# A new order of the same steps on five engines, in a kernel that joins a recurrence to a two-layer network

## Chip, core and metric

One core of a Trainium2 chip runs the kernel. The metric is the device time of one execution in microseconds (us). Engines are named as in the profile: PE is TensorE (matmul) and PEld its weight loads, DVE is VectorE, ACT is ScalarE, POOL is GpSimd, SP issues the transfers.

## What is computed

The recurrence runs over 768 time steps for 4 x 8 heads of width 48, and its output, 3072 tokens of 384 numbers, goes through a two-layer network:

```python
state = np.zeros((B, H, D, D), dtype=np.float32)
for t in range(S):
    kt, vt, rt = (k[:, :, t], v[:, :, t], r[:, :, t])
    cur = np.einsum('bhd,bhe->bhde', u[None] * kt, vt)
    y[:, :, t] = np.einsum('bhd,bhde->bhe', rt, state + cur)
    state = w[None, :, :, None] * state + np.einsum('bhd,bhe->bhde', kt, vt)
...
h = x @ w_in                                         # 3072 x 384 by 384 x 2048
sp = np.maximum(h, 0.0) + np.log1p(np.exp(-np.abs(h)))
return ((h * erf(sp)) @ w_out).astype(np.float32)    # by 2048 x 384
```

## The kernel before

**Tiling.** The recurrence is cut into chunks of 128 time steps: 24 chunks, number g = 4 x (place in the sequence) + batch. Four chunks fill a block of 512 tokens, x. The network takes a block in 16 hidden tiles of 128, so 96 pairs of a first product (f0 to f95) and a second one (p0 to p95). The first two blocks go through hidden tiles 0 to 7 first, then both through 8 to 15. Products are made of three float32r passes (high and low parts), so f and p are 9 matmuls each.

**Order.** Nothing is scheduled by the framework: a string of some 1700 words, ORDER, is read from left to right, and each word issues one step. Each engine runs its own instructions in the order in which they were issued, and waits at an instruction until its inputs are there; buffers are handed out in that order too. A word is a letter, a number and, for some, a part; + at its end puts the step on GpSimd, * on ScalarE, nothing on VectorE.

- For chunk g: L (a, b) issue its two loads on SP (L66, L69). K and R multiply k and r in place by powers of the decay (L187, L191), V turns k on TensorE, N brings it back or multiplies k in its other layout (L195, L208). Q a and b multiply by u and by k (L212, L215), Q c sums to q (L219); M puts q on the diagonal of am for one half (L230 on ScalarE, L232 elsewhere). A is the k-r product (L249), P the masked copies of A into am (L255), Y the chunk's y (L272), D its contribution to the state (L291), S the state's update (a, b add: L303, L305; c, d scale: L309), X the high and low part of y written to the block's x (L312, L315).
- For weights: F fetches a group of 768 columns (two hidden tiles) of the first (0) or second (1) matrix, as 64-bit numbers, into one of two buffers (L102); C a to f make float32 of it and split it into a high and a low part: a, e on ScalarE (L118, L128), b, c, d on VectorE (L120, L122, L125), f the low part (L130). Group 13 is group 3 of the second matrix.
- For pair n: f (L338), a and b two tanh (L345, L349), z (L354), c, d, e (L358, L362, L366), g (L370), h the high part gh (L376), l the low part gl (L381), p (L397). h tiles have three buffers, s1, s2, gh and gl two each.
- W issues dummy matmuls that keep TensorE busy (L87), O moves a finished or interrupted accumulation out (L414 to L425), Z tests whether w lies in the expected range (L435 to L438), for a branch at the end.

The words are read by one loop:

```python
for i, x in enumerate(words):
    eng = {"+": nc.gpsimd, "*": nc.scalar}.get(x[-1], nc.vector)
    what, x = x[0], x.rstrip("+*")
    ...
    if what == "l":
        act_l(num, eng)
```

Of the kernel before, what the change touches and what calls it, by code (L numbers as in the profile page):

```python
# [619 lines left out]
Q6c N6+ z0 M61* M60+ P51 a1 C01f W4 Y5 c0 b1 S3a R6 C02a f2 z1 X5a C02b c1 X5b d0 C02c d1 A6 e0 C02d a2 P61 e1 F03  # L620
C02e g0 W4 D6 b2 P60 C02f+ f3 h0 g1 h1 l0 C11a Y6 z2 a3 C11b c2 C11c b3 f4 X6a S6b d2 l1 e2 C11d p0 a4 S6a S6d+ F12 g2
C11e S6c+ z3 b4 C11f c3 p1 h2 X6b C03a l2 d3 C03b f5 z4 e3 C03c c4 d4 C03d D5 e4 p2 S5a a5 F13 g4 S5c+ C03e S5b g3
S5d+ b5 C03f h3 D4 h4 l3 f6 L7a C12a S4a l4+ S4b z5 L7b c5 C12b f7 a6 S4c C12c d5 L8a b6 R7 e5 K7 L9a p3 a7 C12d b7
Q7a C12e F05 Q7b A7 C12f+ Q7c g5 M71* L9b z6 p4 M70* K9+ P71 L8b c6 K8+ P70 h5 Y7 d6 R9 C13a l5 e6 p5 z7 X7a Q8a+ g6
c7 X7b h6 Q8b d7 f8 l6 e7 C13b g7 N8+ Q8c h7 C13c A9 a8 M80* l7 f9 R8 b8 C13d z8 M81+ C13e F14 f10 c8 C13f a9 d8 Q9a
p6 b9 N7 S4d e8 z9 Q9b+ C05a g8 c9 p7 C05b h8 Q9c d9 N9 C05c O70a e9 f11 O70b M91+ O72a g9 a10 O72b M90+ P91 h9 b10
f12 l8+ P90 a11 O71a b11 l9+ O71b z10 A8 c10 C05d a12 d10 p8 z11 F04 C05e P80 c11 C05f+ P81 e10 Y9 d11 g10 b12 e11 h10
D8 g11 f13 C14a l10+ C14b z12 f14 a13 C14c c12 b13 C14d d12 p9 a14 F15 C14e e12 C14f b14 p10 g12 h11 C04a l11 z13 p11
h12 C04b c13 l12 d13 z14 e13 f15 C04c c14 C04d d14 e14 g13 F06 p12 C04e g14 a15 C04f h13 b15 f16 l13 h14 z15 C15a l14
c15 C15b f17 a16 C15c d15 b16 C15d e15 p13 a17 g15 F07 C15e z16 b17 C15f c16 f18 h15 C06a l15+ d16 p14 a18 z17 e16  # L630
C06b b18 C06c c17 p15 d17 C06d O150a g16 C06e O150b f19 h16 F16 C06f e17 O151a l16+ g17 C07a O151b f20 h17 C07b a19
l17 O152a z18 b19 O152b p16 C07c c18 a20 z19 d18 C07d c19 p17 e18 F17 d19 g18 b20 h18 f21 e19 l18+ C07e g19 h19 C07f+
z20 p18 a21 c20 b21 l19 C16a p19 z21 d20 C16b c21 C16c e20 d21 f22 g20 e21 C16d h20 g21 C16e f23 l20 h21 C16f a22 b22
l21 C17a p20 z22 a23 C17b c22 C17c b23 p21 d22 C17d e22 z23 C17e g22 f24 c23 C17f+ h22 d23 e23 l22 O232a f25 a24 g23
O230a b24 h23 z24 X9a l23 p22 c24 X9b a25 d24 b25 p23 e24 z25 O230b c25 g24 O230c d25 h24 Y8 O232b e25 l24+ O232c g25
f26 X8a S8b S8a h25 S8d+ X8b S8c+ l25+ O231a f27 a26 b26 z26 c26 D7 O231b a27 f28 L10a S7b d26 S7d S7a b27 L11a S7c+
e26 z27 p24 g26 a28 L10b c27 b28 K10 d27 R10+ L11b f29 h26 e27 l26+ g27 O231c p25 a29 z28 b29 R11 c28 K11 d28 Q11a A10
h27 Q11b e28 p26 l27+ Q11c g28 N11+ z29 c29 p27 Q10a h28 Q10b+ d29 e29 l28+ Q10c f30 g29 M101* M100 M110* P101 f31
P100 h29 N10 M111* l29+ a30 A11 a31 b30 p28 P110 b31 z30 z31 c30 P111 c31 Y10 d30 d31 e30 D10 e31 g30 p29 X10a S10b
h30 X10b l30 S10d g31 Y11 O310a S10a h31 O312a S10c l31 p30 X11a X11b f32 f33 a32 b32 z32 f34 c32 a33 d32 b33 p31 e32  # L640
z33 a34 O310b c33 g32 O310c b34 d33 D11 O312b f35 h32 S11b O312c e33 S11d S11a l32+ g33 O311a h33 f36 S11c a35 z34 l33
b35 c34 z35 d34 D9 O311b a36 L12a S9b p32 e34 S9d S9a b36 S9c L12b g34 c35 d35 p33 h34 O311c e35 K12 L13a g35 R12+ f37
h35 L13b Q12a+ L14a l34 A12 a37 Q12b+ z36 b37 L14b p34 c36 R13+ Q12c d36 M120* M121+ f38 K14+ e36 P120 g36 K13+ P121
h36 f39 a38 l35 b38 z37 Q13a c37 A13 N12 a39 l36 d37 p35 Q13b+ z38 b39 e37 R14 c38 g37 p36 N13+ d38 Q13c h37 M131 e38
l37+ P131 f40 g38 M130+ z39 h38 c39 l38+ P130 f41 a40 d39 Q14a b40 Q14b e39 Y13 Q14c a41 N14 b41 z40 g39 D13 c40 p37
S13b X13a S13d d40 X13b e40 S13a S13c g40 f42 h39 l39 z41 f43 c41 a42 d41 b42 Y12 e41 a43 g41 b43 D12 M140* M141+ p38
S12b L15a S12a S12d+ X12a S12c+ X12b L16a A14 h40 L16b l40 f44 K15 L15b z42 R15+ P141 c42 p39 K16+ d42 P140 a44 e42
Q16a+ b44 g42 A15 h41 Q16b l41 p40 R16 z43 N16 c43 Q15a p41 d43 Q16c Q15b+ h42 e43 l42+ Q15c g43 f45 N15+ h43 z44 c44
l43 d44 p42 M150 a45 P150 e44 b45 g44 p43 z45 h44 M151 c45 l44+ P151 d45 e45 Y14 g45 h45 D14 M160 X14a f46 L17a S14a
S14b S14c+ X14b S14d+ L17b M161 l45 A16 a46 b46 f47 P161 R17+ z46 K17+ P160 c46 D15 d46 Q17a+ Y16 a47 e46 Q17b+ b47  # L650
g46 p44 X16a z47 Q17c c47 X16b d47 N17 e47 Y15 h46 g47 l46 p45 X15a L18a S15a S15b M170* S15c+ X15b S15d L18b M171*
A17 h47 p46 P170 l47+ P171 K18+ Y17 Q18a+ R18 p47 X17a Q18b+ X17b O470a N18 O470b O471a Q18c O471b A18 M180 M181+ f48
P180 P181 O472a O472b f49 a48 b48 z48 f50 c48 a49 d48 b49 e48 Y18 z49 a50 g48 c49 h48 D18 d49 l48+ f51 S18b S18a b50
e49 S18c+ z50 X18a g49 c50 p48 X18b a51 S18d d50 b51 h49 f52 e50 l49+ g50 h50 z51 f53 a52 l50+ c51 b52 d51 z52 p49 a53
# [87 lines left out]
```

## Time and profile before

| | us |
|---|---|
| three runs | 529.09, 529.37, 530.21 |
| median | 529.37 |
| span of the profiled execution, first to last instruction | 527.4 |
| median less that span | 1.97 |
| TensorE busy in it | 509.2 (97%) |
| VectorE, ScalarE, GpSimd busy | 350.9, 398.6, 158.7 |

The profiled execution's own time is not listed apart from the three runs; 1.97 us is what lies around the span if it was the median. The page's slices are fortieths of the span, 13.2 us each. In the chain of waits each piece names what held up the next; a line such as L381 is the line of the step, whatever chunk or pair it belongs to.

### The profile page before, as it was taken

Reading aid. Unit: us, or ns where it says so; the run is one execution under the profiler, and the core shown is the slowest. Engines: PE = TensorE matmul, PEld = TensorE weight load, DVE = VectorE, ACT = ScalarE, POOL = GpSimd, SP = SyncE. Lnnn points to the kernel's source line nnn. Section 1 sums busy time; section 2 is a strip of 40 time slices with the busy share of each in tenths; the row PEclk is TensorE's granted clock in tenths of the full one; section 3 lists DMA queues with packets and bytes.
Section 4 is the critical chain, followed back from the end, with each engine's and each line's share of the span. In section 5 each row is a group of like instructions: output and inputs, shape, how many; then the busy total and the mean of one; then the engine's idle time right before and its main releaser. Section 6 shows DMA issues by size and latency. Waiting matters only on the chain.

```text
span 527.4 us, 10451 instructions
## 1 busy us (share of the span) xinstructions
PE 509.2 (97%) x4164; PEld 393.0 (75%) x4164; DVE 350.9 (67%) x610; ACT 398.6 (76%) x765; POOL 158.7 (30%) x147
## 2 busy tenths in 40 slices
...
PEclk9999999999999999999999999999999999999999
...
GB/s 299 315 195 122 121 251 132 112 128 87 155 99 40 236 21 1 188 155 41 137 1 98 139 88 87 2 162 15 35 115 0 2 1 1 16 45 2 0 1 66
DMA packets 13863, 48.91 MB, mean 93 GB/s; under 512 B 1648, under 2 KB 1776, under 8 KB 13808
## 3 DMA queue, kind: packets, MB, share of 16 engines
...
## 4 chain that ended last, share of the span: by engine, by line
PE 79%; DVE 9%; DMA 4%; ACT 3%; POOL 2%; issue 2%; SPq 1%; POOLq 0%; ACTq 0%
PE h L338 34%; PE acc L397 33%; PE y L272 6%; DMA att<-in_att_dram 4%; PE A L249 3%; PE ds L291 1%; DVE s L370 1%; DVE am L255 1%; DVE wt L125 1%; DVE gl L381 1%; POOL gl L381 1%; PE dummy L87 1%; DVE s L354 1%; DVE wt L120 1%; DVE att L191 1%
## 5 line engine op out<-in xcount | busy, mean ns | idle before, releaser
L338 PE MATMUL h<-x,wih 128*128 128x512 f32 x576 | 183.0, 399 | 1.1 <-DVE s L370 1.1
L338 PEld LDWEIGHTS h<-x,wih 128*128 128x128 f32 x576 | 106.6, 188 | 28.5 <-DVE s L370 2.2
L397 PE MATMUL acc<-gh,woh 128*128 128x512 f32 x288 | 116.5, 404 | 1.4 <-ACT woh L128 1.4
L381 POOL TENSOR_TENSOR gl<-s,gh 128x512 fp32r<-128x512 f32 x43 | 56.7, 1321 | 201.0 <-ACT gh L376 200.9
L397 PE MATMUL acc<-gh,wol 128*128 128x512 f32 x288 | 114.0, 396 | 0.8 <-POOL wol L130 0.6
L397 PE MATMUL acc<-gl,woh 128*128 128x512 f32 x288 | 113.8, 395 | 0.2 <-DVE gl L381 0.2
L338 PE MATMUL h<-x,wil 128*128 128x512 f32 x288 | 113.8, 395 | 0.0
L370 DVE SCALAR_TENSOR_TENSOR s<-s,h 128x512 f32<-128x512 f32 x96 | 65.2, 683 | 63.2 <-ACT s L366 62.9
L354 DVE SCALAR_TENSOR_TENSOR s<-s,h 128x512 f32<-128x512 f32 x96 | 65.5, 684 | 53.1 <-ACT s L349 35.4
L376 ACT CAST gh<-s 128x512 fp32r<-128x512 f32 x96 | 59.1, 616 | 34.5 <-DVE s L370 20.7
L358 ACT ACTIVATE s<-s 128x512 f32<-128x512 f32 x96 | 60.2, 629 | 28.7 <-DVE s L354 28.3
L345 ACT ACTIVATE s<-h 128x512 f32<-128x512 f32 x96 | 56.5, 590 | 27.2 <-PE h L338 27.0
L397 PEld LDWEIGHTS acc<-gh,woh 128*128 128x128 f32 x288 | 54.2, 188 | 17.2 <-issue 2.6
L397 PEld LDWEIGHTS acc<-gh,wol 128*128 128x128 f32 x288 | 54.2, 188 | 14.2 <-POOL wol L130 1.0
L338 PEld LDWEIGHTS h<-x,wil 128*128 128x128 f32 x288 | 54.2, 188 | 12.8
L397 PEld LDWEIGHTS acc<-gl,woh 128*128 128x128 f32 x288 | 54.2, 188 | 12.6 <-DVE gl L381 0.8
L349 ACT ACTIVATE s<-s 128x512 f32<-128x512 f32 x96 | 60.0, 626 | 0.9
L362 ACT ACTIVATE s<-s 128x512 f32<-128x512 f32 x96 | 59.8, 627 | 1.0
L366 ACT ACTIVATE s<-s 128x512 f32<-128x512 f32 x96 | 59.7, 626 | 0.8
L381 DVE TENSOR_TENSOR gl<-s,gh 128x512 fp32r<-128x512 f32 x53 | 40.6, 768 | 19.1 <-ACT gh L376 18.8
L255 DVE COPY_PREDICATED am<-mask,A 64x256 f32<-64x256 uint32 x96 | 39.5, 442 | 11.9 <-ACT am L230 4.0
L230 ACT ACTIVATE am<-ident,q 128x128 f32<-128x128 f32 x100 | 30.8, 389 | 3.1 <-DVE q L219 3.0
...
## 6 DMA issues: line engine op xcount, KB each, us to landing
...
```

What stands on the lines that cost most here:

```text
L255: nc.vector.copy_predicated(out=am[r, :, c], data=ap[r, :, c], mask=m[r, hh:hh + 1, c].to_broadcast([r.stop - r.start, NPAIR, H]))
L338: nc.tensor.matmul(out=h, lhsT=w[:, f, q, :], rhs=x[:, xi, q, :], start=k == 0, stop=k == 8)
L345: nc.scalar.activation(out=s1, in_=e["h"], func=AF.Tanh, bias=FB0, scale=FA0)
L349: nc.scalar.activation(out=s1, in_=s1, func=AF.Tanh, bias=FB1, scale=FA1)
L354: nc.vector.scalar_tensor_tensor(out=e["s"], in0=e["s1"], scalar=FG, in1=e["h"], op0=ALU.mult, op1=ALU.add)
L358: nc.scalar.activation(out=s, in_=s, func=AF.Tanh, bias=FB2, scale=FA2)
L362: nc.scalar.activation(out=s, in_=s, func=AF.Square, bias=FB3, scale=FA3)
L366: nc.scalar.activation(out=s, in_=s, func=AF.Square, bias=FB4, scale=FA4)
L370: nc.vector.scalar_tensor_tensor(out=s, in0=s, scalar=FC, in1=ff[n]["h"], op0=ALU.subtract, op1=ALU.mult, reverse0=True)
L376: nc.scalar.copy(out=e["gh"], in_=e["s"])
L381: eng.tensor_tensor(out=e["gl"], in0=e["s"], in1=e["gh"].bitcast(F32), op=ALU.subtract)
L397: nc.tensor.matmul(out=acc[e], lhsT=w[:, f, es], rhs=g, start=first and i == 0, stop=last and i == 2)
```

## The change

The table ORDER is replaced by another one of the same 1723 steps; no function is touched. 134 steps change their engine: 70 from VectorE to GpSimd, 49 from GpSimd to VectorE, 7 from ScalarE to GpSimd, 6 from ScalarE to VectorE, one from GpSimd and one from VectorE to ScalarE. TensorE has the same 283 steps before and now, with the same 62 dummies behind the first 16. Of the diff, which is the table, two lines each way:

```diff
 ORDER = """
-U0 L0a L0b L1a K0 T0 L1b R0 V0 Q0a A0 Q0b+ F00 R1+ Q0c N0* M00* W2 D0 S0b K1+ L2a S0a M01* P00 W5 A1 Q1a L2b P01 Q1b+
-C00a V1 Y0 Q1c N1* C00b M10* F10 K2 D1 R2 V2 M11* P10 L3a S1b Q2a+ P11 Q2b+ S1a L3b W6 Y1 Q2c N2* A2 C00c L4a M21* D2
...
+L0a L0b T0 U0 Q0a+ K0 R0 Q0b L1a W2 V0 K1 L1b L2a Q0c M00 N0* A0 D0 S0b W5 W6 P00 V1 M01* P01 F00 C00a Y0 Q1a+ Q1b+
+Q1c N1* R2 L2b C00b S0a K2 C00c L3a M11* L3b D1 R1+ A1 P11 S1b S1a M10* L4a V2 P10 C00d W6 L4b Q2a+ K3 Q2b+ N2* Q2c R3
...
 """
```

Three places follow, in the instructions as they are issued. The numbers behind att, wt, raw, q, am, s1, s2, h, gh and gl are the chunk, weight group or pair; the last number of a name is the buffer's.

VectorE, from the low part of chunk 7's x to the split of weight group 13 (the second matrix, hidden tiles 6 and 7), before:

```order
L315 TENSOR_TENSOR x1_697<-y7_1142,x1_697 128x3x128
L215 TENSOR_TENSOR att8_1062<-att8_1062 128x384
L381 TENSOR_TENSOR gl_6_1208<-s2_6_1116,gh_6_1194 128x512
L120 TENSOR_SCALAR wt13_1173<-wt13_1173 128x768
L370 SCALAR_TENSOR_TENSOR s2_7_1187<-s2_7_1187,h7_1047 128x512
L219 TENSOR_REDUCE q8_1214<-att8_1062 128x8
L122 SCALAR_TENSOR_TENSOR wt13_1173<-raw13_999,wt13_1173 128x768
L381 TENSOR_TENSOR gl_7_1244<-s2_7_1187,gh_7_1216 128x512
L191 TENSOR_TENSOR att8_1062<-att8_1062,wr_110 112x512
L125 SCALAR_TENSOR_TENSOR wt13_1173<-raw13_999,wt13_1173 128x768
L354 SCALAR_TENSOR_TENSOR s2_8_1259<-s1_8_1237,h8_1198 128x512
L130 TENSOR_TENSOR wol_92<-wt13_1173,woh_91 128x768
```

and now:

```order
L315 TENSOR_TENSOR x1_695<-y7_1114,x1_695 128x3x128
L122 SCALAR_TENSOR_TENSOR wt13_1143<-raw13_976,wt13_1143 128x768
L125 SCALAR_TENSOR_TENSOR wt13_1143<-raw13_976,wt13_1143 128x768
L370 SCALAR_TENSOR_TENSOR s2_6_1051<-s2_6_1051,h6_1015 128x512
L370 SCALAR_TENSOR_TENSOR s2_7_1153<-s2_7_1153,h7_1054 128x512
L130 TENSOR_TENSOR wol_92<-wt13_1143,woh_91 128x768
L381 TENSOR_TENSOR gl_6_1206<-s2_6_1051,gh_6_1201 128x512
L381 TENSOR_TENSOR gl_7_1218<-s2_7_1153,gh_7_1196 128x512
```

The split stands 4 instructions behind x in place of 10: group 13's shift is issued ahead of x, chunk 8's multiplications (L215, L191) have gone to GpSimd, and the two gl stand behind the split.

SP, the loads of chunks 7 to 9 (att) and weight group 05 (raw), before:

```order
L66 DMA att7_1034<-in_att_dram 128x1024
L69 DMA att7_1034<-in_att_dram 128x1216
L66 DMA att8_1062<-in_att_dram 128x1024
L66 DMA att9_1068<-in_att_dram 128x1024
L102 DMA raw05_1085<-in_win_dram 128x768
L69 DMA att9_1068<-in_att_dram 128x1216
L69 DMA att8_1062<-in_att_dram 128x1216
```

and now:

```order
L66 DMA att7_995<-in_att_dram 128x1024
L69 DMA att7_995<-in_att_dram 128x1216
L66 DMA att8_1041<-in_att_dram 128x1024
L69 DMA att8_1041<-in_att_dram 128x1216
L66 DMA att9_1198<-in_att_dram 128x1024
L102 DMA raw05_1220<-in_win_dram 128x768
L69 DMA att9_1198<-in_att_dram 128x1216
```

The second half of chunk 8 has moved from the last of the seven to the fourth.

GpSimd, from chunk 4's first multiplication on, before:

```order
L187 TENSOR_TENSOR att4_384<-att4_384,wk_111 112x512
L212 TENSOR_TENSOR att4_384<-att4_384,ub_85 128x384
L215 TENSOR_TENSOR att4_384<-att4_384 128x384
L212 TENSOR_TENSOR att5_454<-att5_454,ub_85 128x384
L215 TENSOR_TENSOR att5_454<-att5_454 128x384
L195 TENSOR_TENSOR att5_454<-att5_454,wkn_142 128x384
L195 TENSOR_TENSOR att6_538<-att6_538,wkn_142 128x384
L232 TENSOR_TENSOR am6_0_730<-ident_93,q6_720 128x512
L130 TENSOR_TENSOR wil_90<-wt02_775,wih_89 128x768
```

and now, from chunk 5's on:

```order
L191 TENSOR_TENSOR att5_405<-att5_405,wr_110 112x512
L232 TENSOR_TENSOR am4_0_595<-ident_93,q4_491 128x512
L187 TENSOR_TENSOR att5_405<-att5_405,wk_111 112x512
L130 TENSOR_TENSOR wol_92<-wt10_408,woh_91 128x768
L212 TENSOR_TENSOR att6_562<-att6_562,ub_85 128x384
L215 TENSOR_TENSOR att6_562<-att6_562 128x384
L187 TENSOR_TENSOR att6_562<-att6_562,wk_111 112x512
L195 TENSOR_TENSOR att5_405<-att5_405,wkn_142 128x384
L191 TENSOR_TENSOR att6_562<-att6_562,wr_110 112x512
L232 TENSOR_TENSOR am6_0_819<-ident_93,q6_693 128x512
L130 TENSOR_TENSOR wil_90<-wt02_730,wih_89 128x768
L195 TENSOR_TENSOR att6_562<-att6_562,wkn_142 128x384
```

Chunk 5's and 6's k and r, chunk 6's two Q multiplications, the am step of chunk 4 and the split of weight group 10 have come to GpSimd. Elsewhere in the table: GpSimd's k multiplication of chunk 17 (K17) stands two instructions ahead of its am step of chunk 16 (M161); its am step of chunk 9 (M91) stands three ahead of gl 9; the test of w (Z0), which stood behind X23b, now stands between the last pair's second and third output tile; of the last pairs' steps ScalarE has h93 one place earlier and GpSimd has gl 92.

## Rows read from the trace of the kernel before

**Rows 1.** The profile page: busy time of each engine (share of the span, number of instructions), and the TensorE clock that was granted in 40 equal slices (9 is 90% or more).

```profile
PE 509.2 (97%) x4164; PEld 393.0 (75%) x4164; DVE 350.9 (67%) x610; ACT 398.6 (76%) x765; POOL 158.7 (30%) x147
PEclk9999999999999999999999999999999999999999
```

**Rows 2.** Busy time of each engine in stretches: start and end, length, then us busy and instructions of each engine, granted clock, DMA share and GB/s.

```profile
20.00:30.00 10.00, 9.80 (x142) 5.69 (x132) 9.86 (x18) 6.75 (x19) 3.38 (x3) 1.00 0.74 275
40.00:50.00 10.00, 10.00 (x140) 7.24 (x139) 9.43 (x17) 6.52 (x13) 2.02 (x2) 1.00 0.43 154
90.00:100.00 10.00, 8.39 (x36) 6.15 (x35) 9.66 (x14) 8.18 (x17) 2.96 (x2) 1.00 0.24 79
120.00:160.00 40.00, 40.00 (x173) 32.16 (x172) 34.26 (x47) 39.51 (x70) 5.90 (x4) 1.00 0.34 112
```

**Rows 3.** The chain of waits in order of time: start, length, and what the piece is.

```profile
78.78 6.59 DMA att<-in_att_dram
85.43 1.03 POOL att L212
...
94.67 0.96 DVE wol L130
...
114.49 6.28 PE acc L397 x27
...
184.23 1.02 PE A L249 x24
```

**Rows 4.** VectorE's timeline at 15 to 98 us: start, length, line, operation, output and input, shapes; in brackets the idle time before it and what ended it.

```profile
15.90 1.49 DVE L191 TENSOR_TENSOR att<-att,wr 112x512 f32<-112x512 f32 x1
...
27.66 0.54 DVE L219 TENSOR_REDUCE q<-att 128x8 f32<-128x384 f32 x1
...
86.49 0.56 DVE L215 TENSOR_TENSOR att<-att 128x384 f32<-128x384 f32 x1 [1.48 <-POOL att L212]
...
87.57 1.36 DVE L120 TENSOR_SCALAR wt<-wt 128x768 int32<-128x768 int32 x1
...
90.78 1.53 DVE L381 TENSOR_TENSOR gl<-s,gh 128x512 fp32r<-128x512 f32 x1
...
96.59 1.08 DVE L309 TENSOR_TENSOR sbd<-sbd,wp 48x192 f32<-48x192 f32 x1
```

**Rows 5.** TensorE's timeline: the first f, the first matmuls of p6 and the y of chunk 9.

```profile
42.51 0.73 PE L338 MATMUL h<-x,wih 128*128 128x512 f32 x2
...
94.69 0.50 PE L397 MATMUL acc<-gh,woh 128*128 128x512 f32 x1 [1.35 <-ACT woh L128]
...
95.69 0.50 PE L397 MATMUL acc<-gh,wol 128*128 128x512 f32 x1 [0.26 <-DVE wol L130]
...
107.89 0.86 PE L272 MATMUL y<-att,sbd 112*32 112x128 f32 x24 [0.20 <-DVE am L255]
```

**Rows 6.** VectorE's groups of instructions by line and shape, from 0 to 110 us: us busy and mean ns of one, then idle time before them.

```profile
L125 DVE SCALAR_TENSOR_TENSOR wt<-raw,wt 128x768 int32<-128x768 int32 x9 | 9.3, 1038 | 0.1
...
L191 DVE TENSOR_TENSOR att<-att,wr 112x512 f32<-112x512 f32 x9 | 8.0, 893 | 0.1
...
L381 DVE TENSOR_TENSOR gl<-s,gh 128x512 fp32r<-128x512 f32 x7 | 6.0, 855 | 0.0
...
L187 DVE TENSOR_TENSOR att<-att,wk 112x512 f32<-112x512 f32 x6 | 4.1, 682 | 0.1
L212 DVE TENSOR_TENSOR att<-att,ub 128x384 f32<-128x384 f32 x6 | 3.3, 548 | 0.0
L130 DVE TENSOR_TENSOR wil<-wt,wih 128x768 fp32r<-128x768 f32 x3 | 2.8, 950 | 0.0
```

**Rows 7.** Timelines of TensorE, VectorE, SP and GpSimd in the middle: f36 and a state scaling with its neighbour, chunk 22's am step and y, and the load of chunk 17 with the first GpSimd step that had waited for it.

```profile
215.10 1.48 DVE L309 TENSOR_TENSOR sbd<-sbd,wp 48x192 f32<-48x192 f32 x1
...
217.46 0.34 DVE L309 TENSOR_TENSOR sbd<-sbd,wp 48x192 f32<-48x192 f32 x1
...
217.59 0.73 PE L338 MATMUL h<-x,wih 128*128 128x512 f32 x2 [0.86 <-DVE s L370]
...
276.37 0.33 SPq L66 DMA_DIRECT2D att<-in_att_dram  x1
...
280.19 1.29 POOL L191 TENSOR_TENSOR att<-att,wr 112x512 f32<-112x512 f32 x1 [2.31 <-DMA att<-in_att_dram]
...
426.74 0.69 DVE L232 TENSOR_TENSOR am<-ident,q 128x512 f32<-128x512 f32 x1
...
431.68 0.86 PE L272 MATMUL y<-att,sbd 112*32 112x128 f32 x24 [0.77 <-DVE am L255]
```

**Rows 8.** Timelines of TensorE, VectorE and ScalarE: the test of w, and the last pairs' gl, c and p.

```profile
447.10 0.19 PE L437 MATMUL cnt<-bad,mask 112*1 112x4 f32 x2
...
513.01 0.69 DVE L381 TENSOR_TENSOR gl<-s,gh 128x512 fp32r<-128x512 f32 x1 [2.03 <-ACT gh L376]
...
514.52 0.63 ACT L358 ACTIVATE s<-s 128x512 f32<-128x512 f32 x1 [1.01 <-DVE s L354]
...
519.14 0.50 PE L397 MATMUL acc<-gl,woh 128*128 128x512 f32 x1 [0.23 <-DVE gl L381]
```

**Rows 9.** GpSimd's timeline: one multiplication by u and the am step of chunk 8.

```profile
27.71 1.00 POOL L212 TENSOR_TENSOR att<-att,ub 128x384 f32<-128x384 f32 x1 [3.55 <-DMA att<-in_att_dram]
...
90.07 1.69 POOL L232 TENSOR_TENSOR am<-ident,q 128x512 f32<-128x512 f32 x1 [1.55 <-DVE q L219]
```

More of the change, by code (lines that the diff above doesn't have):

```diff
@@ L620 @@
[L620 to L654, printed above, removed]
@@ L675 @@
-d92 f94 l91+ a93 e92 b93 g92 p90 z93 a94 c93 b94 d93 f95 h92 e93 l92 z94 p91 g93 a95 c94 b95 d94 p92 h93 e94 l93 z95
-p93x g94 c95 p93y h94 d95 p93z l94 e95 p94x g95 p94y h95 p94z l95 p95x p95y O950a p95z O950b O951a O951b O952a O952b
+L0a L0b T0 U0 Q0a+ K0 R0 Q0b L1a W2 V0 K1 L1b L2a Q0c M00 N0* A0 D0 S0b W5 W6 P00 V1 M01* P01 F00 C00a Y0 Q1a+ Q1b+
+Q1c N1* R2 L2b C00b S0a K2 C00c L3a M11* L3b D1 R1+ A1 P11 S1b S1a M10* L4a V2 P10 C00d W6 L4b Q2a+ K3 Q2b+ N2* Q2c R3
+Q3a X0a A2 F10 C00e C00f Y1 M20* Q3b L5a R4 C10a C10b M21* W3 W9 W8 W7 Q3c W4 M30* P20 C10c A3 M31* K4+ X0b Q4a+ Q4b+
@@ new lines @@
+P21 Q4c M41* Y2 D2 P30 P31 W4 A4 X1a C10d V3 N3* L5b Q5a+ L6a X1b Q5b+ C10e Y3 X3a Q5c R5+ M51* P41 M40+ P40 S2b M50
+X3b D3 K5+ A5 L6b X2a F01 C10f+ P50 W4 S2a Y4 Q6a+ C01a S3b P51 X2b f0 F02 Q6b+ Q6c X4a M61* C01b S3a C01c C01d f1 X4b
+N4 a0 C01e C01f b0 z0 a1 b1 z1 C02a C02b Y5 X5a X5b F11 f2 c0 d0 C02c C02d c1 e0 g0 d1 K6+ N5+ C02e R6+ A6 P61 e1 W4
+h0 g1 a2 M60+ C02f+ P60 h1 l0 N6+ b2 z2 C11a C11b f3 f4 a3 F03 c2 C11c d2 C11d b3 e2 C11e p0 l1 a4 Y6 g2 C11f F12 z3
+D6 h2 l2+ b4 S6a S6b C03a C03b p1 z4 c3 C03c C03d d3 D5 S5b c4 d4 e4 C03e C03f+ p2 e3 F13 S5a D4 g4 h4 g3 X6a S4b S4a
```

78 lines of the change are left out of this document (55 added, 23 removed).

## The prediction

> **What bounds the kernel now.** I read the page's busy shares and slices first, then the busy times by stretch, the chain of waits, and the timelines at the places where TensorE stands. TensorE is busy for 97% of the span at a full granted clock [rows 1], so only its waits can give time back. They lie early: in every stretch up to 100 us it has gaps or fills with dummy matmuls, while from 120 to 160 us it is busy for 40.00 of 40 us [rows 2]. What makes it wait early is VectorE: 9.86 of 10 us busy in 20:30, 9.43 in 40:50, 9.66 in 90:100. The chain of waits says the same: up to about 108 us it runs through DMA, GpSimd and VectorE steps, and from the long TensorE pieces around 114.49 on it is TensorE nearly to the end [rows 3]. So the case is decided before about 110 us, plus a few single waits later and the end.
>
> The chain shows the early part's worst knot in full. The second half of chunk 8's load is issued late (78.78) and lands 6.59 us later; GpSimd's multiplication by u follows at 85.43, and VectorE, which has the next multiplication in its list, stands idle for it until 86.49; then weight group 13 (shift, or, sign, split at 94.67) comes late, and TensorE's p6 waits for it [rows 3]. VectorE's idle 1.48 us stands in its row [rows 4]; p6 waits 1.35 us for woh and 0.26 us more for wol [rows 5].
>
> **The sum, against the profiled span of 527.4 us.** The TensorE steps are the same 283 in both orders, dummies included, so I count its waits alone.
>
> *Up to chunk 7's y.* VectorE's list ahead of the last masked copy of chunk 7 (P70) loses twelve steps that GpSimd takes: four 384-column multiplications (Q0a, Q1a, Q6a, Q6b) at 0.55, four 512-column ones (R5, K5, K6, R6) at 0.68, one gl (l2) at 0.69, two weight splits (C10f, C03f) at 0.95, one state scaling (S4c) at 0.34: 2.20 + 2.72 + 0.69 + 1.90 + 0.34 = 7.85 us; g5 (0.68) now stands behind P70. It gains Q0b 0.55, K1 0.68 and three am steps (M00, M50, M71) at 0.69: 3.30. Net 8.53 - 3.30 = 5.2 us less, by [rows 6] and, for the am step, the scaling and gl, the rows at 426.74, 217.46 and 513.01 [rows 7, 8].
>
> Against this stands what a GpSimd step does to a VectorE step beside it. At 15.90 us a 512-column multiplication took 1.49 in place of 0.68; the shift at 87.57, the gl at 90.78 and the scaling at 96.59 show 1.36, 1.53 and 1.08, and GpSimd's am step at 90.07 took 1.69 itself [rows 4, 9]. But the reduction at 27.66, beside a GpSimd step of 1.00 us, kept its 0.54 [rows 4, 9]. What is stretched has two operands in SBUF, or is the weight shift; what reads PSUM or one operand is not. GpSimd issues 27 elementwise steps ahead of this point where it issued 21. Price of one, from below: up to 110 us the means of three groups lie above the unstretched ones, 9 x 0.21 (L191), 9 x 0.09 (L125) and 7 x 0.17 (gl) [rows 6], 3.9 us over 32 GpSimd steps, 0.12 each. From above: the three stretched steps of 86 to 97 us lost 0.81 + 0.84 + 0.74 to three GpSimd steps [rows 4], 0.80 each. Ends: 27 at 0.12 is 0.7 us more than 21; half of the 27 at 0.80 (some half of VectorE's steps are not of the stretched kind) is 10.8 against 2.5, 8.3 more. I take the six added steps at 0.80, 4.8 us, since they fall where both engines have work ready, which the 86 to 97 us rows are nearest to. So this stage gives 5.2 - 4.8 = **0.4 us**, between -3.1 and +4.5.
>
> The Trainium skill (SBUF — State Buffer, Who interferes with whom) says that a VectorE instruction with two SBUF inputs and a GpSimd instruction that reads SBUF hold one port in turn, each for its whole length. The stretched rows agree. By that rule alone the six steps would cost their own length, some 1.2 us each, 7.2 in place of 4.8; that is the first rival.
>
> *Chunk 8 and p6 (85 to 97 us).* On SP the two halves of chunk 8 now stand ahead of chunk 9 and of weight group 05, whose wait for VectorE held the queue. On VectorE, Q8b is gone to GpSimd, and ahead of group 13's split there now stand 4 steps behind x1's low part in place of 10. If x1 is ready when it was (85.0), group 13 needs 0.95 + 0.95, the ScalarE rounding 0.84, and the split 0.96: 88.8; two collisions at 0.80 make it 90.4. p6 now stands behind f9 and comes due at about 89.2. It waits 0 to 1.4 us there; before it lost 1.35 + 0.26 and the restarts, about 2.2. I take **1.7 us**, between 0 and 2.2.
>
> *From p7 to 120 us.* Chunk 9's y waited 0.20 us at 107.89 [rows 5], and some pieces around it a little. VectorE's list up to g9 is then 8 us shorter in all, so I take them as gone: **0.4 us**, between -0.5 and +0.9. Behind them GpSimd has a wait added: its am step of chunk 9 needs VectorE's Q9c, and l8 and l9 are queued behind it. They are wanted three to four TensorE steps later, which hides it; without that cover p8 would stand.
>
> *Middle.* f36 waited 0.86 us because VectorE's state scaling (1.48 us) had met a GpSimd gl; chunk 22's y waited 0.77 us, for masked copies that stood behind chunk 22's am step (426.74) and a multiplication of chunk 23 [rows 7]. Both neighbourhoods are ordered anew and both waits go: 1.6 us. New ones come: on GpSimd chunk 17's k multiplication, which waits for a load, now stands ahead of chunk 16's am step. The load was issued at 276.37 and GpSimd could go on at 280.19 [rows 7]; from there 1.3, 0.5 and 1.05 us on GpSimd and 0.9 on VectorE make 7.6 us after chunk 14's ds, where TensorE has p42, f45, A16 and f46, 2.1 + 2.1 + 1.0 + 2.1 = 7.3 (27 matmuls take 6.28, chunk 10's A step 1.02 [rows 3]): a wait of some 0.3. For all others like it I allow 0.5. Net **0.8 us**, between -0.9 and +1.6.
>
> *End.* Behind f95 the chain runs through ScalarE and VectorE: c95 stood 1.01 us for a z95 held behind l93 (513.01), which needs h93; h93 now comes one ScalarE step earlier, and l92 is on GpSimd: about 0.5 us, of which TensorE can use what it waited, 0.23 to 0.5 [rows 8]. The test of w (Z0) now stands between the last two output tiles, so its small matmuls and the reduction behind them sit on the path: about 0.35 us, with 0.19 us for the matmuls at 447.10 [rows 8]. Net **0.1 us**.
>
> Sum: 0.4 + 1.7 + 0.4 + 0.8 + 0.1 = 3.4 us. Span 524.0; with the 2.0 us between span and median, **526.0 us** against 529.37.
>
> Two edits are costed at nothing. Seven am steps go from ScalarE to GpSimd and six to VectorE: ScalarE is busy 6.75 of 10 us in 20:30 and is not what TensorE waits for. Loads of chunks 4 and 5 are issued ahead of weight group 10 and 01: both groups are needed some 10 us after they land; if that cover goes, ScalarE's first step of group 10 holds the am steps of chunks 2 and 3 behind it.
>
> **Rivals.** *Collisions eat it (slower).* Place: weight group 01 (C01b, C01c, C01d) right after f0, where GpSimd now runs K6, N5, R6 and M60 one after the other; f2 needs that group. If each of the four holds VectorE for about its own 1.0 to 1.3 us, and the rest of the stage goes likewise, the extra collisions reach the 8.3 us end: stage one costs 3.1 us, p6 gains nothing, and the middle's new waits eat its old ones: 529.4 + 3.1 = 532.5. It decides where the extra collisions pass some 8 us (4.8 + 3.4). For it: VectorE is busy 9.43 of 10 us in 40:50 [rows 2]; against: GpSimd often waits for loads and stands aside. The skill's rule, carried through, is this rival.
>
> *The waits move (no change).* TensorE's first h needs x of all four chunks, and that chain also runs through loads and am steps. If those end last, VectorE's shorter list only makes it wait: stage one 0, p6 late as before, middle even: 529. For it: at 86.49 it was a load that VectorE waited for [rows 3, 4].
>
> *Few collisions (much faster).* At 0.12 us per GpSimd step stage one gives 4.5, p6 2.2, the next 0.9, middle 1.2, end 0.1: 8.9, or 520.5. For it: GpSimd's steps before collided seldom; against: 27 in place of 21 stand there, where VectorE has no pause.
>
> **Chances.** The measurement of this kernel can tell about 0.2%, 1.06 us, from no change. Forecast case (1.1 to 6 us gained) 0.48, few collisions 0.12, waits move 0.15, collisions eat it 0.25. So faster 0.60, same 0.15, slower 0.25. The range 521.0 to 531.5 leaves out the best of the few-collision case and the worst of the slower one; the forecast case's own range is 523.4 to 528.3.
>
> **What would show it.** Right: VectorE's share in 20 to 100 us still above 90%, with stretched K, R and C steps more numerous than four; no idle time before Q8b or its successors; p6 starting within 1.5 us of f9's end; no wait above 0.5 us between 120 and 500 us. First h at 41.5 to 44.5 us, where it started at 42.5 [rows 5], so hardly earlier; the gain shows only from 85 us on. Wrong: TensorE pure from well before 95 us (few collisions), or f2 more than 2 us behind f1's end and y of chunk 5 (collisions), or waits for GpSimd's gl or am steps above 1 us in the middle.

## The result and the profile after

The changed kernel takes 534.79 us (median of four runs, 533.33 to 536.01) where the kernel before took 529.23: a ratio of 1.010, interval 1.0075 to 1.0125. Forecast were 526.0, faster, and a range of 521.0 to 531.5: the sign is wrong and the time lies outside the range. The profiled execution, the slowest of the four, took 536.01 with a span of 534.3, 6.9 more than the span before, where the medians differ by 5.6.

The page after, as in [rows 1]: busy time by engine, and the granted clock in 40 slices.

```profile
PE 514.1 (96%) x4164; PEld 396.5 (74%) x4164; DVE 357.9 (67%) x594; ACT 396.5 (74%) x721; POOL 199.3 (37%) x174
PEclk9999997999999999999999899999999999999999
```

GpSimd does 40.6 us more, VectorE does 7.0 more although the change takes work from it (8.7 us, an estimate from the shortest instruction of each shape), and TensorE is 4.9 us longer busy with the same 4164 matmuls. Its clock, full throughout before, is down in two slices. The stretches, with the columns of [rows 2]:

```profile
20.00:30.00 10.00, 9.78 (x115) 4.90 (x107) 9.96 (x18) 6.64 (x18) 9.48 (x4) 1.00 0.57 203
40.00:50.00 10.00, 8.51 (x133) 6.84 (x123) 9.83 (x14) 6.41 (x12) 5.02 (x5) 1.00 0.26 80
80.00:90.00 10.00, 6.50 (x67) 5.15 (x68) 9.93 (x12) 6.13 (x11) 6.67 (x6) 0.75 0.04 13
86.00:88.00 2.00, 2.00 (x6) 1.52 (x6) 1.97 (x4) 1.57 (x3) 0.75 (x1) 0.50 0.00 0
90.00:100.00 10.00, 10.00 (x68) 7.75 (x67) 6.75 (x10) 7.76 (x13) 0.21 (x1) 0.91 0.03 12
120.00:160.00 40.00, 40.00 (x221) 31.97 (x221) 32.32 (x46) 38.85 (x67) 8.98 (x8) 1.00 0.35 113
300.00:305.00 5.00, 5.00 (x17) 3.96 (x16) 3.42 (x8) 2.06 (x4) 0.00 (x0) 0.66 0.00 0
```

In 80:90 TensorE loses 3.5 us and the granted clock is 0.75; part of that stretch, of 90:100 and of 300:305 runs at the lower of the two levels, 1.2 GHz (0.50 in 86:88). Both places come behind a wait of TensorE. Where both orders have done the same TensorE steps, their ends compare like this (worked out from the two traces; "before | after" where the last step is not the same; "step" is the gap's growth):

```
last step done      before    after     gap    step
Y7                   83.53    82.53   -1.00   -1.00
f8                   87.92    92.68   +4.76   +5.76
f12                 104.38   106.45   +2.07   -2.69
Y16 | D15           284.10   286.55   +2.45   +0.38
p48 | Y18           311.67   317.56   +5.89   +3.44
p57                 354.29   360.88   +6.59   +0.70
p61 | A21           374.33   382.16   +7.83   +1.24
Y22 | f77           433.42   440.77   +7.35   -0.48
p87                 493.49   500.64   +7.15   -0.20
p95z                521.27   528.73   +7.46   +0.31
```

What follows the last matmul is 0.5 us shorter, which makes the 6.9 of the spans, up to rounding. Three places lose 10.4 us (f8, p48, p61), and the rest gives 3 back. The timeline there, all engines in order of time:

```profile
41.86 2.26 DVE L120 TENSOR_SCALAR wt<-wt 128x768 int32<-128x768 int32 x1
47.35 0.86 PE L272 MATMUL y<-att,sbd 112*32 112x128 f32 x24 [1.49 <-DVE x L315]
...
80.34 1.27 POOL L191 TENSOR_TENSOR att<-att,wr 112x512 f32<-112x512 f32 x1
81.15 3.07 DVE L120 TENSOR_SCALAR wt<-wt 128x768 int32<-128x768 int32 x1
81.58 1.27 POOL L187 TENSOR_TENSOR att<-att,wk 112x512 f32<-112x512 f32 x1
82.82 0.98 POOL L212 TENSOR_TENSOR att<-att,ub 128x384 f32<-128x384 f32 x1
83.88 1.19 POOL L215 TENSOR_TENSOR att<-att 128x384 f32<-128x384 f32 x1
84.14 1.48 DVE L381 TENSOR_TENSOR gl<-s,gh 128x512 fp32r<-128x512 f32 x1
85.67 0.80 PE L397 MATMUL acc<-gl,woh 128*128 128x512 f32 x1 [2.70 <-DVE gl L381]
...
294.61 1.02 POOL L212 TENSOR_TENSOR att<-att,ub 128x384 f32<-128x384 f32 x1
295.66 1.63 DVE L215 TENSOR_TENSOR att<-att 128x384 f32<-128x384 f32 x1 [3.85 <-POOL att L212]
297.21 1.75 DVE L232 TENSOR_TENSOR am<-ident,q 128x512 f32<-128x512 f32 x1
299.61 0.90 PE L338 MATMUL h<-x,wih 128*128 128x512 f32 x2 [1.81 <-DVE s L370]
...
372.55 1.28 POOL L187 TENSOR_TENSOR att<-att,wk 112x512 f32<-112x512 f32 x1
372.60 4.27 DVE L381 TENSOR_TENSOR gl<-s,gh 128x512 fp32r<-128x512 f32 x1 [1.01 <-ACT gh L376]
373.80 2.51 POOL L191 TENSOR_TENSOR att<-att,wr 112x512 f32<-112x512 f32 x2
376.92 0.50 PE L397 MATMUL acc<-gl,woh 128*128 128x512 f32 x1 [1.18 <-DVE gl L381]
```

At 80 us GpSimd runs R9, K9, Q9a, Q9b and R8 one behind the other, since the loads of chunks 8 and 9 are there early and nothing else holds it: in the table these steps stand some 15 us later. VectorE's shift of weight group 13 (81.15) takes 3.07 us, gl 5 behind it 1.48, and p5 waits 2.70. Of the 5.76 us to f8 the other 3.06 is the low clock behind that wait: p5 and f8 have no other wait, and their matmuls take that much longer. At 295 us VectorE stands 3.85 us for GpSimd's Q18a, then both its steps are stretched, g47 is late and f50 waits 1.81; the clock takes 1.6 more. At 372 us gl 61 lasts as long as three GpSimd steps.

VectorE's groups by shape, over the whole run, with the columns of [rows 6], show which instructions this happens to:

```profile
L354 DVE SCALAR_TENSOR_TENSOR s<-s,h 128x512 f32<-128x512 f32 x96 | 65.5, 684 | 40.6 <-ACT s L349 29.9 <-POOL gl L381 9.3 <-POOL att L215 0.5
L381 DVE TENSOR_TENSOR gl<-s,gh 128x512 fp32r<-128x512 f32 x53 | 45.3, 858 | 18.5 <-ACT gh L376 18.3
L232 DVE TENSOR_TENSOR am<-ident,q 128x512 f32<-128x512 f32 x15 | 15.7, 1050 | 0.2
L120 DVE TENSOR_SCALAR wt<-wt 128x768 int32<-128x768 int32 x16 | 14.7, 916 | 3.0 <-ACT wt L118 2.7
L219 DVE TENSOR_REDUCE q<-att 128x8 f32<-128x384 f32 x24 | 13.1, 544 | 0.1
```

gl, am and the shift lie far above their unstretched 0.69, 0.69 [rows 7, 8] and 0.55 us (means before: 768, 697, 636). z (L354), of which one operand is in PSUM, and the reduction keep theirs, 684 and 544.

### The profile page after: what moved, and what is told of

Its sections match the earlier page's. It is cut to its first block, busy times and chain, and to the rows that moved or that the text cites. A ratio compares the mean times of both kernels' runs of the same rounds, so it can differ in the third digit from the quotient of the medians.

```text
span 534.3 us, 10427 instructions
## 1 busy us (share of the span) xinstructions
PE 514.1 (96%) x4164; PEld 396.5 (74%) x4164; DVE 357.9 (67%) x594; ACT 396.5 (74%) x721; POOL 199.3 (37%) x174
## 3 DMA queue, kind: packets, MB, share of 16 engines
HBM read 41.88 MB, written 6.29 MB: 90 GB/s over the span
## 4 chain that ended last, share of the span: by engine, by line
PE 77%; DVE 13%; ACT 4%; issue 2%; DMA 2%; POOL 1%; SPq 0%; DVEq 0%; POOLq 0%; ACTq 0%
PE h L338 33%; PE acc L397 33%; PE y L272 5%; PE A L249 3%; DVE am L255 2%; DVE gl L381 2%; DVE wt L120 2%; PE dummy L87 1%; PE ds L291 1%; DVE s L354 1%; DVE wt L122 1%; ACT gh L376 1%; DMA att<-in_att_dram 1%; ACT s L345 1%; DVE wt L125 1%
## 5 line engine op out<-in xcount | busy, mean ns | idle before, releaser
L338 PE MATMUL h<-x,wih 128*128 128x512 f32 x576 | 184.9, 403 | 2.2 <-DVE s L370 2.2
L338 PEld LDWEIGHTS h<-x,wih 128*128 128x128 f32 x576 | 107.8, 191 | 30.9 <-DVE s L370 3.9
L397 PE MATMUL acc<-gl,woh 128*128 128x512 f32 x288 | 115.1, 400 | 4.1 <-DVE gl L381 4.1
L338 PE MATMUL h<-x,wil 128*128 128x512 f32 x288 | 115.1, 400 | 0.0
L354 DVE SCALAR_TENSOR_TENSOR s<-s,h 128x512 f32<-128x512 f32 x96 | 65.5, 684 | 40.6 <-ACT s L349 29.9
L381 DVE TENSOR_TENSOR gl<-s,gh 128x512 fp32r<-128x512 f32 x53 | 45.3, 858 | 18.5 <-ACT gh L376 18.3
L232 POOL TENSOR_TENSOR am<-ident,q 128x512 f32<-128x512 f32 x19 | 23.5, 1241 | 48.6 <-DVE q L219 48.4
```

Of the source, the lines that this page charges most:

```text
L338: nc.tensor.matmul(out=h, lhsT=w[:, f, q, :], rhs=x[:, xi, q, :], start=k == 0, stop=k == 8)
L354: nc.vector.scalar_tensor_tensor(out=e["s"], in0=e["s1"], scalar=FG, in1=e["h"], op0=ALU.mult, op1=ALU.add)
L381: eng.tensor_tensor(out=e["gl"], in0=e["s"], in1=e["gh"].bitcast(F32), op=ALU.subtract)
L397: nc.tensor.matmul(out=acc[e], lhsT=w[:, f, es], rhs=g, start=first and i == 0, stop=last and i == 2)
```

## The experiments

Ratios are to the kernel before, run on the same chip.

**The changed kernel again**, as the base for the rest.

> The changed kernel once more, so that the others of this call can be compared with it on the same chip. If the low clock behind p5 and behind f50 belongs to the kernel, it shows again in 84 to 92 us and in 300 to 304 us, and the median is 534 to 536 us. If it came by chance, one or both are gone and the median is 531 to 533.

Measured: 534.41 us, 1.0106 (1.0079 to 1.0133). p5 waited 2.71 and f50 1.80 again, and the shift took 3.07 again. Behind f50 the clock was low again; behind p5 it was not this time, and f8 ended 2.5 us sooner for it. The profile still ended only 1.0 us sooner: 1.0 was lost again at p11, whose gl stands behind the split of weight group 14 on VectorE, and at f16, which waited for group 04, and 0.4 behind the last matmul.

```profile
80.00:90.00 10.00, 6.35 (x75) 4.98 (x75) 9.93 (x12) 6.35 (x11) 7.02 (x7) 1.00 0.07 25
```

**gl 6 to GpSimd.**

```diff
-... C13f l6 p6 b8 l7 F05 ...
+... C13f l6+ p6 b8 l7 F05 ...
```

> The changed order with one word changed: gl 6 goes from VectorE to GpSimd, at its place, so that GpSimd waits for gh 6 (about 87 us) ahead of its five multiplications of chunks 8 and 9, which ran one after the other from 80.3 to 86.7 us. VectorE's list up to gl 5 is untouched. Theory A (GpSimd's unbroken run holds VectorE's shift of group 13 and gl 5): the shift takes 0.6 in place of 3.07 us, gl 5 0.7 in place of 1.48, p5 waits under 0.4 in place of 2.70, and the low clock behind it goes too, worth 3.1: 534.8 - 2.4 - 3.1 = 529.3 (528.3 to 530.5). Theory B (VectorE's own list is too long there, gl 5 stands behind too much): p5 waits as before, 534.8 or a little more. Theory C (collision as in A, but the clock falls for another reason): 532.4.

Measured: 534.01, 1.0107 (1.007 to 1.0144). The time is a miss, the mechanism is not: with the run gone from there the shift at 81.00 took 0.55, gl 5 0.69, and p5 did not wait. The run came 9.5 us later and held the next shift, of group 05, instead:

```profile
89.91 3.90 DVE L120 TENSOR_SCALAR wt<-wt 128x768 int32<-128x768 int32 x1 [1.60 <-ACT wt L118]
93.46 1.20 POOL L215 TENSOR_TENSOR att<-att 128x384 f32<-128x384 f32 x1
98.38 0.73 PE L338 MATMUL h<-x,wih 128*128 128x512 f32 x2 [1.34 <-DVE s L370]
```

By the times, the shift got its turn in both kernels only where GpSimd paused before Q9b, which has to wait for its own Q9a. Theory B, VectorE's list alone, is out.

**Filling p5's wait.** The function is new, the word stands between Y7 and C13a.

```diff
+    def fill(n):
+        d = ps1.tile([P, TB], F32, tag="A1", name="fill")
+        for _ in range(n):
+            nc.tensor.matmul(out=d, lhsT=wih[:, 0, 0, :], rhs=xts[0][:, 0, 0, :], start=True, stop=True)
-... p4 Y7 C13a ...
+... p4 Y7 W11+ C13a ...
```

> The changed order, with 11 more matmuls of 128x512 into an unused PSUM bank between chunk 7's y and p5, about 2.56 us of TensorE work that fills the wait for gl 5 and serves nothing else. If the low clock behind p5 follows from TensorE's standing idle: the granted clock is 1.00 from 80 to 100 us, p5 and f8 take 4.6 us in place of 7.7 behind the wait, and the time is 534.8 - 3.1 = 531.7 (530.8 to 532.8). If the clock falls for another reason (what the engines draw together, or by chance): the low stretch stays, 534.8, or up to 0.5 more.

Measured: 533.42, 1.0091 (1.0065 to 1.0117). The clock stayed full:

```profile
80.00:90.00 10.00, 9.32 (x88) 7.42 (x89) 9.93 (x12) 6.09 (x11) 6.42 (x6) 1.00 0.01 4
```

Alone this decides little, since the unfilled wait had shown a full clock once too, and the later waits at p11 and f16 took back part. The time is a miss: 1.0 us less than the changed kernel on the same chip, which is not clear of noise, where 531.7 was expected.

**Q18b back on GpSimd.**

```diff
-... d47 e47 Q18b A17 M171 ...
+... d47 e47 Q18b+ A17 M171 ...
```

> The changed order with one word changed: chunk 18's multiplication Q18b goes from VectorE back to GpSimd, where it was before the change. In the changed kernel VectorE stood 3.85 us idle for GpSimd's Q18a, took 1.63 for Q18b beside GpSimd's K18 and 1.75 for an am step beside R18, and g47 and with it f50 came 1.81 us late; then the clock was 0.66 in 300 to 305 us. Theory A (the wait across the two engines makes f50 late and the low clock follows): f50 does not wait, 534.8 - 1.8 - 1.6 = 531.4 (530.7 to 532.3). Rival (g47 is late for e47, which ScalarE ends at 296.5, or the am step collides anyway): at most 0.8 gained, 534.0 to 534.8.

Measured: 530.96, 1.0041 (1.0016 to 1.0066), 3.45 less than the changed kernel. f50 starts without a wait, the clock is full there, and in the trace the step to f50 gives 3.41. Theory A's 3.4 holds to a tenth.

```profile
300.00:305.00 5.00, 5.00 (x58) 3.95 (x60) 2.56 (x6) 3.25 (x7) 0.18 (x1) 1.00 0.13 52
```

**Three multiplications back on VectorE.**

```diff
-... p7 O71a O71b R9+ c9 d9 e9 K9+ Q9a+ Q9b+ R8+ Q9c M91+ ...
+... p7 O71a O71b R9 c9 d9 e9 K9+ Q9a Q9b+ R8 Q9c M91+ ...
```

> The changed order with three multiplications of chunks 8 and 9 (R9, Q9a, R8) back on VectorE, each at its place in the table. GpSimd's run of seven steps that need nothing but loads (78.9 to 86.7 us) is then cut: Q9b has to wait for VectorE's Q9a, and R8 and R9 are gone; VectorE takes them behind g8, where it stood idle. Theory A (the unbroken run holds VectorE): neither group 13's shift nor group 05's is held (0.6 to 1.2 us in place of 3.07, and of the 3.90 that group 05's shift took when gl 6 delayed the run), p5 waits under 0.5, f11 and p6 under 0.5 together: against 534.4 of the changed kernel in the last call 2.7 less wait, part of the low clock, and no give-back behind: 530.5 (529 to 531.7). Theory B (VectorE's list is the limit, 1.9 us more work makes it worse): 534.4 to 536.

Measured: 533.87, 1.0081 (1.0046 to 1.0115): a miss. Both shifts are short (0.86 and 0.56), p5, p6 and f11 do not wait. But R9 stood behind g8, and A9 waited for it, and the clock fell behind that wait:

```profile
94.86 1.09 PE L249 MATMUL A<-att 48*64 48x128 f32 x32 [1.97 <-DVE att L191]
```

**Four places mended**: the two edits above, `K21+ h61 l61` to `h61 l61+ K21+`, and Z0 from the end to behind X23b.

> The changed order with four places mended: R9, Q9a, R8 back on VectorE (p5), Q18b back on GpSimd (f50), gl 61 on GpSimd ahead of K21, R21, R20 instead of on VectorE beside them (p61, gl 61 took 4.27 us there), and the test of w back behind chunk 23's x (the end). If these four places are the whole of what the change lost: 534.4 - 3.9 - 3.4 - 1.2 - 0.3 = 525.6 (524 to 527.5), under the kernel before (528.6 in the last call). If the chip takes back what one place gives at the next late step (as group 14 and 04 did when gl 6 moved): 528 to 530.

Measured: 531.80, 1.0057 (1.0035 to 1.008), above both forecasts. p61 no longer waits (1.44 in the trace), A9 waits 2.02 for R9 as in the last one, and Z0's new place was a mistake of mine: VectorE stood for the small matmul behind TensorE's queue, and g78 to p79 came late.

```profile
451.32 0.15 DVE L438 TENSOR_REDUCE fi<-cnt 1x1 int32<-1x4 f32 x1 [3.05 <-PE cnt L437]
458.99 0.50 PE L397 MATMUL acc<-gl,woh 128*128 128x512 f32 x1 [0.92 <-POOL gl L381]
```

**Bursts on GpSimd in the kernel before**, three kernels. A word behind b85 and one behind b89 add four multiplications each.

```diff
+        elif what == "B":
+            n, chain = num % 100, num // 100
+            s1 = ff[n]["s1"]
+            o = apool.tile([P, AW], F32, tag="att", name=f"burst{n}")
+            for k in range(4):
+                dst = o[:, 0:TB] if chain else o[:, k * TB:(k + 1) * TB]
+                nc.gpsimd.tensor_tensor(out=dst, in0=dst if chain and k else s1, in1=s1, op=ALU.mult)
-... b85 g84 z85 ... b89 g88 ...
+... b85 B085 g84 z85 ... b89 B189 g88 ...
```

> The kernel before, with eight idle multiplications (128x512, two operands in SBUF, results unused) added on GpSimd near its end, where GpSimd is free: four behind b85 that do not depend on each other, and four behind b89 of which each reads what the one ahead of it wrote. gl 84 (VectorE) becomes ready inside the first four, gl 88 inside the second four; both took 0.69 us before. Theory A (VectorE waits for a pause between GpSimd instructions, and independent ones leave none): gl 84 takes 4.0 to 5.0 us, to the end of the four, gl 88 0.8 to 2.0. Theory A2 (they take turns, instruction by instruction): both 1.0 to 2.0. Theory A3 (they share at half speed each): both 1.2 to 1.5, and GpSimd's multiplications are stretched. z85, which reads PSUM, keeps its 0.68 in all three. The time: 4 us more by A at p84, 529 to 530 by the others.

A single run, 530.18. gl 84 took 0.73 (it asked 0.18 before the first of the four ended), gl 88 1.68 in the chain, z85 0.68. Theory A as put there failed.

The second kernel reads `s1[:PR]` and `wk` in place of s1 twice:

> The two bursts again, with two different operands (the decay powers as the second), as the kernel's own multiplications have them: four independent multiplications behind b85, four in a chain behind b89. In the first try gl 84 slipped in where the first of four ended (0.73 us), and gl 88 took 1.68 beside a chained one. Theory A (a run without a pause holds VectorE to its end, a chain lets it in after one instruction): gl 84 3.5 to 5, gl 88 1.0 to 2.0. Theory A2 (one GpSimd instruction at most is waited for): both under 2.0; then the 3 and 4 us of the changed kernel need another reason.

A single run, 533.35, with early waits of 1.74 and 2.08 us (at 18 and 35 us) that have nothing to do with the bursts: gl 84 asked in the first of four and had its turn behind it, and the second multiplication was stretched. The chained burst missed gl 88.

```profile
477.42 6.04 POOL L510 TENSOR_TENSOR burst<-s,wk 112x512 f32<-112x512 f32 x4 [3.66 <-ACT s L349]
478.29 0.98 DVE L381 TENSOR_TENSOR gl<-s,gh 128x512 fp32r<-128x512 f32 x1
```

The third has in-place multiplications, and a VectorE shift behind z89:

> The kernel before with two bursts of four GpSimd multiplications near its end, of which the last three work in place on parts of a tile that do not depend on each other, as the kernel's k and r multiplications do, and with an added VectorE shift of 128x768 behind z89, inside the second burst (its result is not used). Theory A (an in-place run without a pause holds VectorE to its end): gl 84 and the shift both 3.5 to 5 us. Theory S (the shift is what is held long): gl 84 under 2.0, the shift 3 to 5. Theory A2 (one instruction at most): gl 84 under 2.0, the shift under 1.9; then what held gl 61 for three instructions stays open.

A single run, 532.39: gl 84, the shift and the gl behind it each waited for one GpSimd step (theory A2). So a single turn is the rule in these bursts, and what held gl 61 for three is open.

```profile
477.11 0.99 DVE L381 TENSOR_TENSOR gl<-s,gh 128x512 fp32r<-128x512 f32 x1
495.48 1.09 DVE L513 TENSOR_SCALAR burst<-burst 128x768 int32<-128x768 int32 x1
496.49 1.78 DVE L381 TENSOR_TENSOR gl<-s,gh 128x512 fp32r<-128x512 f32 x1
```

**The early engine moves undone**, on top of the four mended places.

```diff
-Q0a+ Q1a+ Q6a+ Q6b+ R5+ K5+ K6+ R6+ l2+ C10f+ C03f+ S4c+ Q0b  K1  M00  M50  M71
+Q0a  Q1a  Q6a  Q6b  R5  K5  K6  R6  l2  C10f  C03f  S4c  Q0b+ K1+ M00* M50* M71*
```

> The four mended places as in the kernel with them, and besides the early engine moves undone: the twelve steps Q0a, Q1a, Q6a, Q6b, R5, K5, K6, R6, l2, C10f, C03f and S4c back on VectorE, Q0b and K1 back on GpSimd, three am steps (M00, M50, M71) back on ScalarE; the order stays. This measures the first term of the sum by itself. As the sum had it (5.2 us of relief less 4.8 of collisions): 0.4 slower than with them. If the collisions cost little: up to 4.5 slower. If they cost more than the relief, as at C01's shift (2.26 us) now: 0.5 to 3 faster than with them.

Measured: 546.03, 1.0321 (1.0286 to 1.0356), 14.2 more than with them; outside all three. Chunk 7's y ends 10.9 us later than in the changed kernel, and A6 alone waits 5.22, because K6 and R6 stand late in VectorE's list (R6 ends at 59.74):

```profile
59.84 1.97 PE L249 MATMUL A<-att 48*64 48x128 f32 x32 [5.22 <-issue]
```

The new order is made for these engines, so this does not measure my term by itself; it shows that the moves do serve this order.

**Mended, second version**: Q18b and gl 61 as above, Q9a and R8 on VectorE, R9 behind l7, Z0 left at the end.

```diff
-... b8 l7 F05 ... O71b R9 c9 d9 e9 K9+ Q9a Q9b+ R8 Q9c ...
+... b8 l7 R9 F05 ... O71b c9 d9 e9 K9+ Q9a Q9b+ R8 Q9c ...
```

> The changed order with Q18b on GpSimd and gl 61 on GpSimd ahead of K21 as before, Q9a and R8 on VectorE as before, but R9 on VectorE already behind gl 7, where VectorE stood 0.65 us idle, and the test of w left at the end. In the kernel with four mended places the product A9 waited 2.02 us for R9, which stood behind g8, and the test of w behind chunk 23's x made VectorE stand 3.05 us for a small matmul, so that p79 and f84 lost 1.8. If these two account for what was given back there: 531.8 - 2.0 - 1.8 + 0.3 = 528.3 (527 to 529.5). If a late step behind takes it back again (p11 and f16 with groups 14 and 04, which are wanted 0.8 us before they come): 529.5 to 531.

Measured: 528.76, 1.0012 (0.9991 to 1.0034). Three places mended bring the whole loss back, although f13, p11 and f16 give back 2.0 in the trace and p63 0.8. Against the kernel before, this order is 4.0 us ahead behind f12, where 2.5 was forecast (0.4 + 1.7 + 0.4), and 0.3 at the last matmul: without the three places the early gain comes, and later waits use it up.

**The early run cut as well.**

```diff
-... z1 C02a C02b ... d1 K6+ N5+ C02e R6+ A6 ... C02f+ P60 ...
+... z1 R6 C02a C02b ... d1 K6+ C02e A6 ... C02f+ N5+ P60 ...
```

> As e9_mended_2, and the run of GpSimd steps that holds group 01's shift (2.26 us from 41.86) and its or step (1.53) cut: R6 on VectorE behind z1, N5 behind the split C02f, so that GpSimd stops behind K6 for VectorE's q of chunk 6. Theory A (hold by an unbroken run): the shift takes 0.6 to 0.9, chunk 5's y waits under 0.7 in place of 1.5, and 0.8 to 1.6 of it reach the end: 1.2 under e9_mended_2. If VectorE's list is the limit there (R6 adds 0.69): within 0.5 of it, or slower.

Measured: 528.52, 0.9987 (0.9956 to 1.0018), no difference from the kernel before that can be told. The shift took 0.55 in place of 2.26 and chunk 5's y did not wait; of the 1.6 this gave there, 0.6 was left at chunk 7's y, and of the 1.2 expected at the end 0.2 came.

```profile
41.47 0.55 DVE L120 TENSOR_SCALAR wt<-wt 128x768 int32<-128x768 int32 x1
```

**Chunk 17's product three times**, which fills f50's wait in the changed kernel.

```diff
-        for p in range(NPAIR):
+        for p in list(range(NPAIR)) * (3 if g == 17 else 1):
```

> The changed kernel with chunk 17's k-r product computed three times into the same PSUM banks: some 2.0 us more TensorE work exactly where f50 waits 1.81 us (and has shown a low clock behind the wait in every profile so far). Nothing else needs the product before 299.7. If the low clock follows from TensorE standing idle: f50 and p46 run at 1.00, and the time is the changed kernel's less 1.6, plus up to 0.5 for what the products take beyond the wait: 534.4 - 1.3 = 533.1 (532.5 to 533.8). If the clock falls there for another reason: 534.4 to 535.

Measured: 533.60, 1.0092 (1.0061 to 1.0123), inside the range of the first theory; 0.8 less than the changed kernel, which ran on another chip, is not clear of noise. In the profiles it is: from the start of chunk 17's product to the end of p46 7.35 us pass, in both profiles of the changed kernel 8.9. With some 1.8 us more of useless work in the wait the clock stays full, where it was 0.66 without:

```profile
295.35 2.84 PE L249 MATMUL A<-att 48*64 48x128 f32 x96
300.00:305.00 5.00, 5.00 (x33) 3.86 (x35) 2.07 (x5) 2.83 (x6) 0.00 (x0) 1.00 0.03 11
```

## Why the prediction was wrong

**Up to chunk 7's y: net nearly right, by two errors.** 0.4 us were forecast, 1.0 came. I took 4.8 us of extra collisions from ends of 0.7 and 8.3. VectorE instructions stretched by over 0.25 us up to P70's end were 4 before, with 2.2 us in sum, and 10 now, with 8.4: 6.2 extra, more than the relief of 5.2. My count of GpSimd's steps was off too: ahead of P70 the tables hold 26 for 23, not 27 for 21, but by time 31 had begun for 23 when P70 ended, since GpSimd ran ahead of its places. Eight more at 0.80 make 6.4 (an estimate), so the price was good and the number was not. What saved the stage is a term that I left out: VectorE stood idle less. It is busy 7.24 and 9.80 us in the first two stretches of 10 us, where it was 6.29 and 8.95, 1.8 more.

**Chunk 8 and p6: the step that failed.** "Two collisions at 0.80 make it 90.4. [...] I take 1.7 us": I watched p6 and group 13's split, and p6's wait did go, though f9 ahead of it now ended late. But I priced GpSimd's steps at their places in the table. With chunk 8's load moved ahead GpSimd ran its five multiplications at once, ahead of p5, and one of them after the other held one shift. The 2.70 us wait at p5 is not in the sum, nor is the 3.06 of low clock behind it. From Y7 to f12, which also holds the term "from p7 to 120 us", 2.1 was forecast as a gain and 3.07 was lost.

**The middle: right on the waits that I named, wrong on the allowance.** f36 and chunk 22's y start without a wait, and K17 ahead of M161 cost nothing. "For all others like it I allow 0.5": f50 alone cost 3.4 (Q18b moved to VectorE behind GpSimd's Q18a), p61 1.2, the stretch with chunk 17's ds, which waited 0.31, 0.7. The sign that I had put down, a wait above 0.5 us between 120 and 500 us, came at f50 (1.81) and p61 (1.18). Forecast +0.8; from f12 to p87 it lost 5.1. That one word, Q18b, is shown to be worth 3.45.

**The end**: 0.1 forecast as a gain, 0.3 lost up to the last matmul; p95x still waits 0.23 for its gl, and the matmuls of the test stand in between. What follows was 0.5 shorter here, but lasts from 5.5 to 6.3 us in the profiles of the changed kernel and its variants, so it is not counted to the change.

**The rival** that came out is the slower one, in sign and nearly in time (532.5 for 534.8), given 0.25. Its place was wrong: the collision at group 01 came (2.26 us at 41.86), and cost y of chunk 5 its 1.49, but the stage absorbed it. Up to chunk 7's y the 6.2 us lie between my 4.8 and its 7.2, and its point of decision (8 us extra) was not reached: the loss came where one long hold met a TensorE step with no slack. That its time came so near is in part luck. "The skill's rule, carried through" was too mild in one way: it took a hold for one GpSimd step, and gl 61 waited for three (4.27 us). The Trainium skill (SBUF — State Buffer, Who interferes with whom) says that whoever issues first has the shared port pair for the whole instruction; the trace agrees that one side stands while the other runs, but the wait here was longer than one instruction.

**Range and chances.** The rows that I priced from lost 0.74 to 0.84 us each [rows 4], the state scaling 1.1 [rows 7], and none showed a low clock; the range ends at 531.5, below the slower rival's own 532.5. One row of the trace before that I passed over had a longer hold: an r multiplication (L191 at 293.12) took 2.48 us beside two GpSimd steps in a row.

```profile
292.80 1.29 POOL L187 TENSOR_TENSOR att<-att,wk 112x512 f32<-112x512 f32 x1
293.12 2.48 DVE L191 TENSOR_TENSOR att<-att,wr 112x512 f32<-112x512 f32 x1
294.04 1.01 POOL L212 TENSOR_TENSOR att<-att,ub 128x384 f32<-128x384 f32 x1
```

**Open**: why some holds last one GpSimd step and others two or three, though they come again in each profile of the same order (3.06 to 3.08 at group 13 in five of five). The holds of 2.48, 3.07 and 3.90 us ended where GpSimd paused 0.08 us ahead of a Q b that needs its own Q a, that of gl 61 with the end of GpSimd's run; the one at 41.86 ended at neither, and in the added bursts VectorE got in without a pause. Why p11 and f16 wait as soon as the stage ahead is faster is read from the traces (groups 14 and 04 come late) and was not tried.
